# One linear-attention and two-MoE kernel: weight pieces pinned on GpSimd's queue, half of the next x split in place, g's affine moved to y's eviction

## The chip, the cores and the metric

One Trainium2 chip (trn2), one NeuronCore. The metric is device time of one execution in microseconds, given as the median of several runs. Lower is better.

## The reference, cut to what matters

```python
q_s = softmax(q, axis=-1)                 # per token and head, 4 x 8 x 576 x 64
k_s = softmax(k, axis=2)                  # over the sequence
kv  = einsum('bhsd,bhse->bhde', k_s, v)
x   = einsum('bhsd,bhde->bhse', q_s, kv)  # to 2304 tokens x 512
h   = x @ moe_w_in                        # 512 -> 2048
r   = maximum(h, 0)
g   = s * (r * r) + b                     # s and b are single numbers
x2  = g @ moe_w_out                       # 2048 -> 512
h2  = x2 @ moe2_w_in
out = (h2 * tanh(softplus(h2))) @ moe2_w_out
```

The weights come as float64, so the kernel first makes float32 of their bit halves. Products are made in float32r, each operand cut into a high and a low part (`split`: a cast on ScalarE, a subtraction on VectorE), with three matmuls for one product (`passes`).

## The kernel before, in words

**First MoE.** The tokens are cut into five chunks (512, 256, 512, 512, 512), and a step is one chunk c and one of 16 blocks f of 128 hidden units. In each step TensorE makes h of the step two ahead (`emit_h`, 12 matmuls), ScalarE makes r, r², and s·r²+b in three instructions (`emit_relu2`, L233 to L237) and splits g, and TensorE adds 12 matmuls into the four banks of y (`emit_y`). After 16 steps `y_out` copies y to SBUF and stores it to DRAM (yd). The attention for the next chunk, with its loads of kb, vb and q on SP's queue (SyncE), runs among these steps.

**Preparing the second MoE's weights.** The second MoE multiplies pairs of chunks, (0, 2) and (3, 4), by a scheme with seven products P1 to P7 in place of eight, and chunk 1 plainly (the rest). It needs sums of weight blocks, split into high and low. That is done during chunks 2 to 4 in 32 units: `unit_load` fetches 512 KB of raw weights into ur (one buffer, L288, on GpSimd's queue, the profile's POOL); `unit_sums` makes float32 of it (`bits`: ACT L128, then DVE L129, L132, L136, L140), starts the next unit's load, and forms the block sums (L299); `unit_split` splits them into umem and stores them to DRAM (wdi for w_in, wdo for w_out, POOL L312). ACT's instruction L128 and the casts are held in program order with ACT's relu L233 (`keep_in_program_order`); the rest of the order is chosen by a scheduler that simulates the program.

**Second MoE.** For a pair, `b_load` fetches the y blocks, `b_sums` makes the seven inputs x of P1 to P7 and splits them. For pair 0 this is done in place (`put_slot`), for pair 1 through DRAM (`put_dram` stores, `x_get` fetches 1 MB per product at L375). Then eight `h_unit` (42 matmuls each, s sums L436, mish L439), and `y_pair`, which goes over the seven products, each with eight blocks F. The split weights come from DRAM in pieces of up to 1 MB through a ring of three buffers (`ring_load`, tile rw, POOL L395 and L398): a piece is asked for when the one three before it has been used. `rest_load` (L563, L566) fetches the pieces for chunk 1. All these loads are on POOL's queue, in the order that the scheduler gives them. An instruction that issues a DMA waits there for its buffer, and what stands behind it waits too.

Of the kernel before, what the change touches and what calls it, by code (L numbers as in the profile page):

```python
# [31 lines left out]
def kernel(  # L32
# [191 lines left out]
    def emit_relu2(m):  # L224

        n = CHUNKS[steps[m][0]]
        if whole_y(m):
            r = gp.tile([P, CM], F32, tag="gl", name=f"r{m}")[:, 0:n]
            g_t[m] = (None, r)
        else:  # L230
            r = rp.tile([P, CM], F32, tag="r", name=f"r{m}")[:, 0:n]
            g_t[m] = g_tiles(m, n)
        op = nc.scalar.activation(out=r, in_=h_ps.pop(m), func=AF.Relu)  # L233
        if m >= U0:
            tc.keep_in_program_order(op)
        nc.scalar.activation(out=r, in_=r, func=AF.Square)
        nc.scalar.activation(out=r, in_=r, func=AF.Identity, scale=sb_s, bias=sb_b)  # L237
        if not whole_y(m):
            split(*g_t[m], r)

    def emit_y(n):
# [6 lines left out]
        for m in range(NK):  # L248
            ps = y_ps[c][m][:, 0:nt]
# [6 lines left out]
    def y_out(c):  # L256
        w = CHUNKS[c]
        for m, ps in enumerate(y_ps.pop(c)):
# [19 lines left out]
    def unit_load(e):  # L278
# [38 lines left out]
    events = [(fn, e) for e in range(len(units)) for fn in (unit_sums, unit_split)]  # L317

    def unit_event(i):
        fn, e = events[i]  # L320
        fn(e)

# [593 lines left out]
    for n in range(NS):  # L916
# [111 lines left out]
```

## Time and profile before

| | |
|---|---|
| median of 3 runs | 911.91 us (909.95 to 914.84) |
| the profiled execution | 908.81 us, span 907.0 us |
| TensorE (PE) busy | 839.7 us, 93% of the span |
| VectorE (DVE) busy | 619.2 us, 68% |
| ScalarE (ACT) busy | 491.6 us, 54% |
| GpSimd (POOL) busy | 130.7 us, 14% |
| DMA | 186.36 MB, mean 205 GB/s |
| mean granted TensorE clock | 0.981 |

By time: up to 30 us the first loads, chunk 0 to about 141 us, chunk 1 to 208, chunk 2 to 322, chunk 3 to 419, chunk 4 to 526; pair 0's `h_unit`s to 598, its `y_pair` to 683; pair 1's to 767 and 847; the rest to 907. A busy PE includes matmuls at half clock, so the shares are read with the granted clock and with the number of matmuls that started in a stretch.

### The profile page before, as it was taken

To read this page: it belongs to the slowest core of one execution; us is meant where nothing else is said; L and a number is where in the kernel's file an instruction comes from. 1 tells how busy PE (TensorE), PEld (TensorE's weight loads), DVE (VectorE), ACT (ScalarE), POOL (GpSimd) and SP (SyncE) were. 2 spreads that over 40 slices of the span, in tenths; PEclk is the share of its full clock that TensorE was granted. 3 is DMA by queue.
4 is the path that set the end of the run, shared out by engine and by line. 5 is a ranking of instruction groups with operands and counts; after the bars stand their busy time and mean duration, and the time that the engine had idled before them with its cause. 6 is when DMAs were issued, how large, how long until landed. Compare 5 with 4: busy or idle time off the path is not lost.

```text
span 907.0 us, 11652 instructions
## 1 busy us (share of the span) xinstructions
PE 839.7 (93%) x4084; PEld 667.4 (74%) x4084; DVE 619.2 (68%) x1147; ACT 491.6 (54%) x864; POOL 130.7 (14%) x212
## 2 busy tenths in 40 slices
PE   4799998999999898998988988987999999699998
PEld 3344887998877677786865777776788888578897
DVE  7888987666777866676669667864865656386511
ACT  4666886776667765675667644443443333344422
POOL 4000000000112122222221201120011112000110
PEclk9999999999999899999999999998999999899999
DMA  7992123123655466667674599997556768955791
GB/s 198 326 379 59 34 73 110 52 63 99 209 178 179 137 239 233 210 196 248 205 226 148 180 327 323 360 401 272 173 189 217 213 196 262 352 185 186 229 304 47
DMA packets 87498, 186.36 MB, mean 205 GB/s; under 512 B 27152, under 2 KB 45328, under 8 KB 82960
## 3 DMA queue, kind: packets, MB, share of 16 engines
q0 software_dynamic: 33968, 133.18, 45.2%
q1 hardware_dynamic: 52384, 51.40, 17.8%
q10 hardware_dynamic: 1088, 1.05, 0.4%
q8 instruction: 32, 0.52, 0.2%
q14 instruction: 26, 0.21, 0.1%
HBM read 135.27 MB, written 50.33 MB: 205 GB/s over the span
## 4 chain that ended last, share of the span: by engine, by line
PE 45%; DMA 21%; DVE 18%; issue 7%; ACT 7%; POOL 1%; SPq 1%; POOLq 0%; ACTq 0%; DVEq 0%
PE P L176 15%; PE h L176 6%; DMA ur<-in_moe_w_in_dram 5%; PE y L176 4%; DMA rw<-wdo 4%; PE h L212 4%; DMA ur<-in_moe_w_out_dram 4%; PE y L252 3%; PE rh L176 3%; PE ry L176 2%; DVE u L140 2%; DVE u L136 2%; DVE g L340 2%; DMA b<-yd 2%; ACT u L128 1%
## 5 line engine op out<-in xcount | busy, mean ns | idle before, releaser
L176 PE MATMUL h<-xh,w 128*128 128x512 f32 (+1 forms) x568 | 180.0, 382 | 13.9 <-ACT r L233 13.3
L176 PE MATMUL y<-gh,w 128*128 128x512 f32 (+1 forms) x584 | 177.1, 370 | 0.9 <-ACT gh L169 0.9
L176 PE MATMUL P<-xoP,rw 128*128 128x512 f32 x672 | 157.0, 391 | 6.9 <-DMA rw<-wdi 5.6
L176 PEld LDWEIGHTS P<-xoP,rw 128*128 128x128 f32 x672 | 125.1, 188 | 35.2 <-issue 5.6
L176 PEld LDWEIGHTS h<-xh,w 128*128 128x128 f32 x568 | 106.6, 194 | 36.6 <-ACT r L233 17.7
L169 ACT CAST ghy_P<-g 128x512 fp32r<-128x512 f32 x112 | 69.7, 623 | 104.0 <-DVE gly_P L166 34.7
L176 PEld LDWEIGHTS y<-gh,w 128*128 128x128 f32 x584 | 106.5, 189 | 20.2 <-ACT gh L169 2.2
L166 DVE TENSOR_TENSOR gly_P<-g,ghy_P 128x512 fp32r<-128x512 f32 x112 | 76.2, 690 | 60.5 <-ACT ghy_P L169 59.8
L176 PE MATMUL y<-gl,w 128*128 128x512 f32 (+1 forms) x292 | 106.8, 368 | 0.8 <-DVE gl L166 0.8
L176 PE MATMUL h<-xl,w 128*128 128x512 f32 (+1 forms) x284 | 106.6, 376 | 0.6 <-DVE xl L166 0.6
L176 PE MATMUL P<-ghy_P,rw 128*128 128x512 f32 x224 | 89.5, 401 | 14.4 <-DMA rw<-wdo 14.4
L436 DVE TENSOR_TENSOR s<-s,P 128x512 f32<-128x512 f32 x112 | 74.7, 685 | 39.5 <-PE P L176 28.0
L439 ACT ACTIVATE g<-s 128x512 f32<-128x512 f32 x64 | 39.8, 632 | 76.2 <-DVE s L436 75.7
L176 PEld LDWEIGHTS y<-gl,w 128*128 128x128 f32 x292 | 55.0, 188 | 10.3 <-DVE gl L166 1.6
L176 PEld LDWEIGHTS h<-xl,w 128*128 128x128 f32 x284 | 55.3, 195 | 9.7 <-DVE xl L166 1.0
L237 ACT ACTIVATE r<-r,sb_b,sb_s 128x512 f32<-128x512 f32 (+1 forms) x80 | 60.8, 770 | 1.4
L176 PEld LDWEIGHTS P<-ghy_P,rw 128*128 128x128 f32 x224 | 43.3, 193 | 24.4 <-issue 15.9
L166 DVE TENSOR_TENSOR gl<-r,gh 128x512 fp32r<-128x512 f32 (+1 forms) x73 | 45.6, 628 | 20.4 <-ACT gh L169 20.1
L169 ACT CAST umem<-u 128x512 fp32r<-128x512 f32 x64 | 37.3, 618 | 37.7 <-DVE u L299 32.7
L233 ACT ACTIVATE r<-h 128x512 f32<-128x512 f32 (+1 forms) x80 | 43.0, 549 | 20.8 <-PE h L176 14.3
L288 POOL DMA_DIRECT2D ur<-in_moe_w_in_dram x16 | 11.7, 734 | 270.2 <-DVE u L299 124.6
L166 DVE TENSOR_TENSOR umem<-u,umem 128x512 fp32r<-128x512 f32 x64 | 42.2, 688 | 12.3 <-ACT umem L169 12.1
(180 smaller groups left out, 1400.5 us busy)
## 6 DMA issues: line engine op xcount, KB each, us to landing
rw<-wdo POOLq DMA_DIRECT2D x28, 1024.0 KB, 5.1
wdi<-umem POOLq DMA_DIRECT2D x32, 512.0 KB, 4.0
rw<-wdi POOLq DMA_DIRECT2D x16, 1024.0 KB, 6.8
wdo<-umem POOLq DMA_DIRECT2D x32, 512.0 KB, 4.3
rw<-wdi POOLq DMA_DIRECT2D x16, 768.0 KB, 6.8
raw<-in_moe_w_in_dram SPq DMA_DIRECT2D x16, 512.0 KB, 9.9
raw<-in_moe_w_out_dram SPq DMA_DIRECT2D x16, 512.0 KB, 10.7
ur<-in_moe_w_in_dram POOLq DMA_DIRECT2D x16, 512.0 KB, 4.6
```

Source lines behind the costliest of these rows:

```text
L136: nc.vector.scalar_tensor_tensor(out=ti, in0=high, scalar=-0x40000000, in1=ti, op0=ALU.bitwise_and, op1=ALU.bitwise_or,)
L140: nc.vector.scalar_tensor_tensor(out=ti, in0=low, scalar=29, in1=ti, op0=ALU.logical_shift_right, op1=ALU.bitwise_or,)
L166: eng.tensor_tensor(out=lo, in0=src, in1=hi.bitcast(F32), op=ALU.subtract)
L169: pin(nc.scalar.copy(out=hi, in_=src))
L176: mm = nc.tensor.matmul(out=ps, lhsT=x, rhs=y, start=start, stop=stop)
L212: nc.tensor.matmul(out=h_ps[m], lhsT=wl[:, o], rhs=x_whole[kk], start=kk == 0, stop=kk == NK - 1,)
L233: op = nc.scalar.activation(out=r, in_=h_ps.pop(m), func=AF.Relu)
L237: nc.scalar.activation(out=r, in_=r, func=AF.Identity, scale=sb_s, bias=sb_b)
L252: nc.tensor.matmul(out=ps, lhsT=wl[:, o], rhs=gl, start=f == 0, stop=False)
L340: nc.vector.tensor_tensor(out=t.rearrange("p (a b) n -> p b a n", b=2)[:, 1], in0=t[:, 1:3], in1=t[:, 0:1].to_broadcast([P, 2, CM]), op=AL ...
L436: nc.vector.tensor_tensor(out=out, in0=a, in1=b, op=ALU.add)
L439: nc.scalar.activation(out=g[:, spot], in_=src, func=AF.Mish)
```

## The change

1. The units' raw loads go from GpSimd's queue to SP's. A unit's sums and its split are placed half a step apart, and the units evenly in half steps (slots "early" at the start of a step and "unit" at its end).
2. `ring_load`, `rest_load` and the load in the new `put_both` are held in program order on POOL's queue.
3. Pair 1's x: only k block 0 goes through DRAM (3.5 MB written and read in place of 7). k block 1 is split in place by `put_both`, one product at a time after each product of pair 0's `y_pair` in the program text; that function also fetches block 0's half (512 KB).
4. ACT's instruction s·r²+b (L237) goes. y's eviction multiplies by s, and adds b times a column sum of w_out: for chunk 1, g is made two columns of ones wider, so that y's bank has the column sums in two more columns; from these `bsum` is taken. Chunks 1 to 4 add it at eviction, chunk 0 in `b_steps` of pair 0 (four DVE instructions).

```diff
+    bsum = const.tile([P, NK], F32, name="bsum")
...
-            r = rp.tile([P, CM], F32, tag="r", name=f"r{m}")[:, 0:n]
-            g_t[m] = g_tiles(m, n)
+            wide = n + (2 if steps[m][0] == 1 else 0)
+            full = rp.tile([P, CM], F32, tag="r", name=f"r{m}")[:, 0:wide]
+            r = full[:, 0:n]
+            g_t[m] = g_tiles(m, wide)
+            if wide > n:
+                nc.gpsimd.memset(full[:, n:wide], 1.0)
         op = nc.scalar.activation(out=r, in_=h_ps.pop(m), func=AF.Relu)
         if m >= U0:
             tc.keep_in_program_order(op)
         nc.scalar.activation(out=r, in_=r, func=AF.Square)
-        nc.scalar.activation(out=r, in_=r, func=AF.Identity, scale=sb_s, bias=sb_b)
         if not whole_y(m):
-            split(*g_t[m], r)
+            split(*g_t[m], full)
...
         for m in range(NK):
-            ps = y_ps[c][m][:, 0:nt]
+            ps = y_ps[c][m][:, 0:nt + (2 if c == 1 else 0)]
...
-            (nc.vector.tensor_copy if m % 2 else nc.scalar.copy)(out=ys, in_=ps[:, 0:w])
+            b = bsum[:, m:m + 1]
+            if c == 1:
+                nc.vector.tensor_scalar(out=b, in0=ps[:, w:w + 1], scalar1=sb_b, scalar2=None, op0=ALU.mult)
+            if c == 0:
+                nc.scalar.activation(out=ys, in_=ps[:, 0:w], func=AF.Copy, scale=sb_s)
+            elif m % 2:
+                nc.vector.tensor_scalar(
+                    out=ys, in0=ps[:, 0:w], scalar1=sb_s, scalar2=b, op0=ALU.mult, op1=ALU.add
+                )
+            else:
+                nc.scalar.activation(out=ys, in_=ps[:, 0:w], func=AF.Identity, scale=sb_s, bias=b)
             nc.sync.dma_start(out=y_dram[c][:, m, :], in_=ys)
...
-    x_dram = {r: dram.tile([P, 2, 2, CM], F32, name=f"xd{r}") for r in H_ORDER}
+    x_dram = {r: dram.tile([P, 2, CM], F32, name=f"xd{r}") for r in H_ORDER}
...
-        nc.gpsimd.dma_start(out=raw.rearrange("p (j f) -> p j f", j=2), in_=src)
+        nc.sync.dma_start(out=raw.rearrange("p (j f) -> p j f", j=2), in_=src)
...
+    def b_steps(pair, kb, put):
         t = b_raw.pop(kb)
-        put("P1", kb, t[:, 0])
-        diff3(t)
-        put("P7", kb, t[:, 3])
-        put("P2", kb, t[:, 1])
-        sum2(t)
-        put("P6", kb, t[:, 0])
-        diff41(t)
-        put("P5", kb, t[:, 3])
-        put("P4", kb, t[:, 1])
-        put("P3", kb, t[:, 2])
-
-    def x_slot(r):
-        x_op[r] = wp.tile([P, 2, 2, CM], F32R, tag=f"w{H_ORDER.index(r)}", name=f"xo{r}")
+        if pair == 0:
+            for spot in range(2):
+                b = bsum[:, 2 * spot + kb:2 * spot + kb + 1]
+                nc.vector.tensor_scalar(out=t[:, spot], in0=t[:, spot], scalar1=b, scalar2=None, op0=ALU.add)
+        for r in Y_ORDER:
+            if r == "P7":
+                diff3(t)
+            elif r == "P6":
+                sum2(t)
+            elif r == "P5":
+                diff41(t)
+            put(r, kb, t[:, SPOT[r]])
+            yield
+
...
-            nc.sync.dma_start(out=x_dram[r][:, i, kb], in_=t.bitcast(F32))
-
-    def x_get(r):
-        x_slot(r)
-        nc.gpsimd.dma_start(out=x_op[r], in_=x_dram[r])
+            nc.sync.dma_start(out=x_dram[r][:, i], in_=t.bitcast(F32))
+
+    def put_both(r, kb, src):
+        x_op[r] = wp.tile([P, 2, 2, CM], F32R, tag=f"w{H_ORDER.index(r)}", name=f"xo{r}")
+        pin(nc.gpsimd.dma_start(out=x_op[r][:, :, 1 - kb], in_=x_dram[r]))
+        split(x_op[r][:, 0, kb], x_op[r][:, 1, kb], src)
...
-            nc.gpsimd.dma_start(out=t[:, :, 0:o.stop - o.start], in_=wi_dram[a][:, :, o])
+            pin(nc.gpsimd.dma_start(out=t[:, :, 0:o.stop - o.start], in_=wi_dram[a][:, :, o]))
         else:
             t = t.rearrange("p i f h d -> p (i f h d)")
-            nc.gpsimd.dma_start(out=t, in_=wo_dram[b][:, BLOCK[a]].rearrange("p f i h d -> p (f i h d)"))
+            pin(nc.gpsimd.dma_start(out=t, in_=wo_dram[b][:, BLOCK[a]].rearrange("p f i h d -> p (f i h d)")))
...
-            nc.gpsimd.dma_start(out=t, in_=wi_dram[F][:, :, 3:7])
+            pin(nc.gpsimd.dma_start(out=t, in_=wi_dram[F][:, :, 3:7]))
...
-    for i in range(len(events)):
-        at(U0 + i * (U1 - U0) // len(events), "unit", unit_event, i)
+    for e in range(len(units)):
+        i = 2 * (U1 - U0) * e // len(units)
+        for d, fn in enumerate((unit_sums, unit_split)):
+            at(U0 + (i + d) // 2, ("early", "unit")[(i + d) % 2], fn, e)
     for kb in range(2):
         at(L0 + 8, "load", b_load, 0, kb, f"w{NU + kb}")
-        at(L0 + 10 + kb, "unit", b_sums, kb, put_slot)
+        at(L0 + 10 + kb, "unit", b_all, 0, kb, put_slot)
...
-            elif F in (1, 3, 5):
-                if F > 1:
-                    b_sums(F // 2 - 1, put_dram)
-                if F < 5:
-                    b_load(1, F // 2, "w7")
+            elif F in (1, 5):
+                b_load(1, F // 4, "w7")
+            elif F == 3:
+                b_all(1, 0, put_dram)
         if pair == 0:
-            more = [(x_get, r) for r in H_ORDER]
+            steps_b = b_steps(1, 1, put_both)
+            more = [(next, steps_b)] * 7
```

**POOL's queue, start of pair 0's `y_pair`.** rw is a ring piece (here of wdo), xoP the x of pair 1; the names' numbers are buffers. Before:

```order
L398 DMA rw_5368<-wdo_101 128x2048
L375 DMA xoP_5538<-xdP_103 128x2048
L375 DMA xoP_5632<-xdP_104 128x2048
L375 DMA xoP_5724<-xdP_105 128x2048
L398 DMA rw_5406<-wdo_102 128x2048
L375 DMA xoP_5818<-xdP_106 128x2048
L375 DMA xoP_5910<-xdP_107 128x2048
L375 DMA xoP_6002<-xdP_108 128x2048
L398 DMA rw_5438<-wdo_101 128x2048
L375 DMA xoP_6092<-xdP_109 128x2048
```

With the change:

```order
L411 DMA rw_5268<-wdo_102 128x2048
L411 DMA rw_5306<-wdo_103 128x2048
L411 DMA rw_5338<-wdo_102 128x2048
L411 DMA rw_5392<-wdo_103 128x2048
L411 DMA rw_5436<-wdo_102 128x2048
L387 DMA xoP_5438<-xdP_104 128x2x512
```

Six xoP loads of 1 MB that stood between the first three pieces are gone from there; the first piece of x, now of half the size, stands behind the fifth.

**POOL's queue, start of pair 1's `y_pair`.** rw_wi and rw_wo are the rest's pieces. Before:

```order
L398 DMA rw_6626<-wdo_101 128x2048
L563 DMA rw_wi_6815<-wdi_93 128x2x1024
L563 DMA rw_wi_6909<-wdi_94 128x2x1024
L563 DMA rw_wi_7095<-wdi_95 128x2x1024
L398 DMA rw_6671<-wdo_102 128x2048
L566 DMA rw_wo_7001<-wdo_101 128x4x512
L566 DMA rw_wo_7187<-wdo_101 128x4x512
L563 DMA rw_wi_7277<-wdi_96 128x2x1024
L398 DMA rw_6703<-wdo_101 128x2048
L398 DMA rw_6769<-wdo_102 128x2048
```

With the change:

```order
L411 DMA rw_6543<-wdo_102 128x2048
L411 DMA rw_6588<-wdo_103 128x2048
L411 DMA rw_6620<-wdo_102 128x2048
L411 DMA rw_6686<-wdo_103 128x2048
L411 DMA rw_6730<-wdo_102 128x2048
L576 DMA rw_wi_6732<-wdi_94 128x2x1024
L411 DMA rw_6780<-wdo_103 128x2048
L411 DMA rw_6824<-wdo_102 128x2048
L576 DMA rw_wi_6826<-wdi_95 128x2x1024
```

Six of the rest's pieces that stood ahead of the third ring piece stand behind later ones, one after two ring pieces.

**SP's queue, start of chunk 2, with the change.** ur is a unit's raw weights; kb, vb, q are the attention's loads, yd stores y. Before, the same loads stand in the same queue without the ur, which stood on POOL's.

```order
L647 DMA kb<-in_k_dram 128x2x256
L280 DMA yd_90<-ys_1_2135 128x256
L651 DMA kb<-in_k_dram 64x2x64
L667 DMA vb<-in_v_dram 128x4x64 x2
L302 DMA ur_2220<-in_moe_w_in_dram 128x2x512
L671 DMA vb<-in_v_dram 64x2x64
L302 DMA ur_2340<-in_moe_w_in_dram 128x2x512
L685 DMA q_3_2605<-in_q_dram 112x2x256
L685 DMA q_3_2605<-in_q_dram 16x2x256
L647 DMA kb<-in_k_dram 128x2x256
L651 DMA kb<-in_k_dram 64x2x64
L302 DMA ur_2421<-in_moe_w_in_dram 128x2x512
```

A ur now stands behind loads that wait for the attention's buffers.

**DVE, around pair 0's last `h_unit`.** s_0_7 are its seven sums, gly_P_3 the low part that the fourth block of `y_pair`'s first product needs. Before:

```order
L436 TENSOR_TENSOR s_0_7_5371<-s_0_7_5370,P_0_7_5382 128x512
L436 TENSOR_TENSOR s_0_7_5372<-s_0_7_5371,P_0_7_5390 128x512
L436 TENSOR_TENSOR s_0_7_5371<-s_0_7_5371,P_0_7_5398 128x512
L436 TENSOR_TENSOR s_0_7_5370<-s_0_7_5370,P_0_7_5408 128x512
L436 TENSOR_TENSOR s_0_7_5370<-s_0_7_5372,P_0_7_5398 128x512
L436 TENSOR_TENSOR s_0_7_5372<-s_0_7_5372,P_0_7_5417 128x512
L436 TENSOR_TENSOR s_0_7_5371<-s_0_7_5371,P_0_7_5428 128x512
L334 TENSOR_TENSOR g_7_5373<-g_7_5373 128x512
L166 TENSOR_TENSOR gly_P_3_5482<-g_3_4998,ghy_P_3_5481 128x512
```

With the change (the first 12 of 18 rows up to gly_P_3; the other six are three xoP subtractions, the last sum, a difference of g, and gly_P_3; L345 and L348 on b_1 are the sum and the difference that L337 and L340 were):

```order
L449 TENSOR_TENSOR s_0_7_5271<-s_0_7_5270,P_0_7_5282 128x512
L167 TENSOR_TENSOR xoP_5438<-b_1_5195,xoP_5438 128x512
L345 TENSOR_TENSOR b_1_5195<-b_1_5195 128x512
L449 TENSOR_TENSOR s_0_7_5272<-s_0_7_5271,P_0_7_5290 128x512
L167 TENSOR_TENSOR xoP_5726<-b_1_5195,xoP_5726 128x512
L449 TENSOR_TENSOR s_0_7_5271<-s_0_7_5271,P_0_7_5298 128x512
L167 TENSOR_TENSOR xoP_5535<-b_1_5195,xoP_5535 128x512
L449 TENSOR_TENSOR s_0_7_5270<-s_0_7_5270,P_0_7_5308 128x512
L167 TENSOR_TENSOR xoP_5629<-b_1_5195,xoP_5629 128x512
L348 TENSOR_TENSOR b_1_5195<-b_1_5195 128x2x512
L449 TENSOR_TENSOR s_0_7_5270<-s_0_7_5272,P_0_7_5298 128x512
L449 TENSOR_TENSOR s_0_7_5271<-s_0_7_5271,P_0_7_5328 128x512
```

Seven subtractions for xoP, one sum and one difference of b, nine instructions, now stand among the seven sums ahead of gly_P_3.

## Rows read from the trace of the kernel before

**Rows 1.** By stretch: busy us (instructions) of PE, PEld, DVE, ACT, POOL; granted clock, DMA share, GB/s.

```profile
144.00:208.00 64.00, 61.84 (x529) 58.64 (x528) 41.30 (x104) 44.30 (x105) 0.00 (x0) 1.00 0.28 76
419.00:526.00 107.00, 96.23 (x399) 76.18 (x399) 74.57 (x148) 67.82 (x112) 24.53 (x33) 0.97 0.63 204
683.00:767.00 84.00, 84.00 (x383) 69.48 (x382) 49.37 (x76) 27.82 (x46) 16.01 (x24) 1.00 0.73 210
```

**Rows 2.** PE's waits over the whole run: us in total, times, longest us.

```profile
PE P L176 <- DMA rw<-wdo: 14.4, 4, 5.1
PE h L176 <- ACT r L233: 13.3, 11, 3.6
...
PE P L176 <- DMA rw<-wdi: 5.6, 3, 2.4
PE x L176 <- DVE qtl L166: 3.9, 1, 3.9
```

**Rows 3.** The chain of waits, 369 to 378 us: start, us, what.

```profile
369.74 4.29 DMA ur<-in_moe_w_out_dram
...
374.11 0.68 ACT u L128
...
376.46 0.70 DVE u L140
...
377.20 0.52 issue
377.73 4.30 DMA ur<-in_moe_w_out_dram
```

**Rows 4.** DMA issues: KB each, median us from issue to landing.

```profile
ur<-in_moe_w_out_dram POOLq DMA_DIRECT2D x16, 512.0 KB, 4.3
...
out_dram<-os SPq DMA_DIRECT2D x8, 512.0 KB, 3.0
...
rx<-yd SPq DMA_DIRECT2D x1, 512.0 KB, 6.1
```

**Rows 5.** By stretch, as rows 1, for 10 us each.

```profile
420.00:430.00 10.00, 6.43 (x22) 4.82 (x21) 6.16 (x14) 5.03 (x9) 2.24 (x3) 0.85 0.78 267
480.00:490.00 10.00, 8.69 (x37) 6.50 (x36) 10.00 (x19) 5.95 (x11) 0.71 (x1) 1.00 0.30 96
592.00:602.00 10.00, 10.00 (x46) 8.28 (x45) 5.47 (x10) 3.16 (x6) 4.20 (x8) 1.00 1.05 393
```

**Rows 6.** Groups of instructions by line, ACT, 208 to 526 us: busy us, mean ns.

```profile
L237 ACT ACTIVATE r<-r,sb_b,sb_s 128x512 f32<-128x512 f32 x48 | 38.3, 812 | 0.8
```

**Rows 7.** Timeline of PE: start, us, line, instruction [idle before, releaser].

```profile
494.22 0.50 PE L176 MATMUL h<-xh,w 128*128 128x512 f32 x1 [2.46 <-ACT r L233]
```

**Rows 8.** The chain of waits, 590 to 630 us.

```profile
598.76 18.08 DMA rw<-wdo
```

**Rows 9.** By stretch, as rows 1, start of both y_pairs.

```profile
600.00:610.00 10.00, 7.74 (x35) 6.09 (x34) 7.11 (x12) 3.73 (x6) 0.53 (x1) 1.00 1.07 427
610.00:620.00 10.00, 4.89 (x16) 3.68 (x15) 1.92 (x3) 2.31 (x5) 0.53 (x1) 0.73 1.09 420
620.00:630.00 10.00, 10.00 (x42) 8.12 (x42) 5.21 (x7) 4.26 (x7) 0.53 (x1) 0.93 0.51 184
770.00:780.00 10.00, 5.30 (x17) 3.97 (x16) 4.36 (x7) 1.61 (x3) 0.54 (x1) 0.75 1.20 407
780.00:790.00 10.00, 7.69 (x31) 5.92 (x30) 4.00 (x6) 3.71 (x7) 0.53 (x1) 0.90 1.14 414
```

**Rows 10.** Timeline of DVE, as rows 7.

```profile
601.93 1.38 DVE L166 TENSOR_TENSOR gly_P<-g,ghy_P 128x512 fp32r<-128x512 f32 x2 [1.29 <-ACT ghy_P L169]
```

**Rows 11.** SP queue's own waits: us in total, times, longest us.

```profile
SPq L672 <- DVE qn L740: 91.5, 11, 18.4
SPq L654 <- PE kv L760: 50.2, 10, 16.3
...
SPq L634 <- DVE ke L717: 35.9, 7, 17.3
```

More of the change, by code (lines that the diff above doesn't have):

```diff
@@ L227, in emit_relu2 @@
         if whole_y(m):
-            r = gp.tile([P, CM], F32, tag="gl", name=f"r{m}")[:, 0:n]
+            r = full = gp.tile([P, CM], F32, tag="gl", name=f"r{m}")[:, 0:n]
             g_t[m] = (None, r)
         else:
-            r = rp.tile([P, CM], F32, tag="r", name=f"r{m}")[:, 0:n]
-            g_t[m] = g_tiles(m, n)
+            wide = n + (2 if steps[m][0] == 1 else 0)
[4 more added lines that the diff above has]
+                nc.gpsimd.memset(full[:, n:wide], 1.0)
         op = nc.scalar.activation(out=r, in_=h_ps.pop(m), func=AF.Relu)
@@ L315, in unit_split @@
             )
[L317 to L321, printed above, removed]
     b_raw, x_op = {}, {}
@@ L343, in diff41, with b_all @@
         )
-    def b_sums(kb, put):
+    def b_steps(pair, kb, put):
         t = b_raw.pop(kb)
-        put("P1", kb, t[:, 0])
-        diff3(t)
-        put("P7", kb, t[:, 3])
-        put("P2", kb, t[:, 1])
-        sum2(t)
-        put("P6", kb, t[:, 0])
-        diff41(t)
-        put("P5", kb, t[:, 3])
-        put("P4", kb, t[:, 1])
-        put("P3", kb, t[:, 2])
-    def x_slot(r):
-        x_op[r] = wp.tile([P, 2, 2, CM], F32R, tag=f"w{H_ORDER.index(r)}", name=f"xo{r}")
+        if pair == 0:
[11 more added lines that the diff above has]
+            yield
+    def b_all(pair, kb, put):
+        for _ in b_steps(pair, kb, put):
+            pass
     def put_slot(r, kb, src):
         if kb == 0:
-            x_slot(r)
+            x_op[r] = wp.tile([P, 2, 2, CM], F32R, tag=f"w{H_ORDER.index(r)}", name=f"xo{r}")
         split(x_op[r][:, 0, kb], x_op[r][:, 1, kb], src)
@@ L370, in put_dram @@
         for i, t in enumerate((hi, lo)):
-            nc.sync.dma_start(out=x_dram[r][:, i, kb], in_=t.bitcast(F32))
-    def x_get(r):
-        x_slot(r)
-        nc.gpsimd.dma_start(out=x_op[r], in_=x_dram[r])
+            nc.sync.dma_start(out=x_dram[r][:, i], in_=t.bitcast(F32))
+    def put_both(r, kb, src):
+        x_op[r] = wp.tile([P, 2, 2, CM], F32R, tag=f"w{H_ORDER.index(r)}", name=f"xo{r}")
+        pin(nc.gpsimd.dma_start(out=x_op[r][:, :, 1 - kb], in_=x_dram[r]))
+        split(x_op[r][:, 0, kb], x_op[r][:, 1, kb], src)
     ring, ring_at = [], [0, 0]
@@ L562, in rest_load @@
         if z == "wi":
-            nc.gpsimd.dma_start(out=t, in_=wi_dram[F][:, :, 3:7])
+            pin(nc.gpsimd.dma_start(out=t, in_=wi_dram[F][:, :, 3:7]))
         else:
             t = t.rearrange("p i b h d -> p (i b h d)").rearrange("p (b i h d) -> p b i h d", b=4, i=2, h=2)
-            nc.gpsimd.dma_start(
+            pin(nc.gpsimd.dma_start(
                 out=t.rearrange("p b i h d -> p b (i h d)"),
                 in_=wo_dram[F // 4][:, 3:7, F % 4].rearrange("p b i h d -> p b (i h d)"),
-            )
+            ))
             t = t.rearrange("p b i h d -> p i b h d")
@@ L922 @@
         boundary = any(steps[m][1] == 0 for m in hs)
-        run(n, "att5", "att2", "att3")
+        run(n, "att5", "att2", "att3", "early")
         if n < NF:
```

## The prediction

> **What bounds the kernel now.** I read the time by stretch first, then TensorE's waits, then the chain of waits in the stretches that lose time. PE is busy nearly throughout, and in pair 1's h_units it has no idle time at all [rows 1]. So the kernel is bounded by matmuls plus the stretches where PE starves, and only these can give time. A full 10 us holds 46 matmuls of 512 columns (592 to 602) [rows 5], that is 0.217 us each. PE's waits name three kinds of starving [rows 2].
>
> First, ring pieces: PE waits for rw<-wdo 14.4 us in four waits, two at the start of each y_pair, and 5.6 us in three waits for rw<-wdi in pair 0's h_units. Second, the relu of the next step: 13.3 us in 11 waits. Third, one wait of 3.9 us on the attention's qtl.
>
> The second kind comes from the weight units. In chunks 3 and 4 the chain of waits runs round a loop [rows 3]: ur is fetched in 4.29 us, one ACT and four DVE instructions take it to 377.20, and 0.52 us after these comes the next fetch, 8.0 us after the last. There is one ur buffer, so no fetch starts earlier. 32 units are spread over 45 steps of 24 matmuls, so a unit has 45/32 x 24 x 0.217 = 7.3 us where nothing else runs. The loop is slower than that. The unit falls behind, ACT's L128 waits for ur in its fixed place, and the relu stands behind it. Where PE waits long, the granted clock then falls: 420 to 430 us holds 22 matmuls instead of 46, at a clock of 0.85 [rows 5].
>
> **The change part by part.** The sum is made against the profiled execution, 908.8 us, which is 3.1 us under the median of 911.9 that the forecast is scaled to.
>
> *ur on SP's queue.* Removed: 32 issues on POOL. Added: 32 issues on SP, among the loads of kb, vb and q and the y stores. No row shows this transfer on SP. The nearest rows bound it: 512 KB on SP landed in 3.0 us (out_dram<-os) and in 6.1 us (rx), against 4.3 us for ur on POOL [rows 4]. I take 3.2, nearer the first, since that is a median of eight and the other a single one. The loop then takes 8.0 - 4.3 + 3.2 = 6.9 us, below 7.3, and the units keep pace. Of the 13.3 us of relu waits one of 2.5 us, at 494 [rows 7], lies behind a stretch in which DVE is 10.00 us busy out of 10 [rows 5]. The other 10.8 us go. In the clock I count 2.5 us: the stretch 420 to 430 lost 24 matmuls, 5.2 us, of which at most 3.6 us is its wait, so 1.6 us is slow matmuls, and one other wait was long enough for something like it. The qtl wait lies among the same crowd of unit work on DVE; I count half, 2.0 us. Total 15.3 us.
>
> *L237 removed.* 48 instructions, 38.3 us, leave ACT in chunks 2 to 4 [rows 6]. ACT is 67.8 of 107 us busy in chunk 4 [rows 1], so nearly all of it is off the path and costs nothing now; it shortens the time from h to gh. Four additions of bsum come into the DVE-full stretch near 480. The loop's two short DVE instructions of the same shape take 377.20 - 374.11 = 3.1 us less 0.68 (ACT) and two of 0.70, so 0.5 us each [rows 3]; four make 2.0 us. That stretch costs PE 4.5 us: 37 matmuls instead of 46 from 480 to 490 [rows 5], 2.0 us, and the wait of 2.5 us after it [rows 7]. I count 2.0 us of it gained net of the additions, since the unit and relu work comes earlier, and keep 0 and 4 as ends. The eviction is still one instruction for each bank.
>
> *Columns of ones.* 12 matmuls in each of 16 steps, 192, are 258 wide instead of 256: 192 x 2/512 x 0.217 = 0.2 us lost. The 16 memsets go to POOL, which is 0.00 us busy in chunk 1 [rows 1]; nothing as long as no other work stands there.
>
> *Pinned ring pieces.* The chain at 598.76 waits 18.08 us for a piece that was issued behind six xoP loads of 1 MB [rows 8], and pair 1's start looks alike with rest pieces in their place. Full stretches would hold 138 and 92 matmuls in the 30 and 20 us shown; there are 93 and 48 [rows 9]. So 45 x 0.217 = 9.8 us and 44 x 0.217 = 9.6 us are lost, waits and half-clock matmuls together. With the pieces first in the queue nothing of 1 MB stands ahead of the second and third piece, and I take both losses back. What is late next in pair 0 is DVE, below.
>
> *k block 1 split in place.* Removed: 14 stores of 256 KB on SP's queue and half of the seven xoP loads. In pair 0's h_units, where PE waited 5.6 us for rw<-wdi, I count two of the three waits, 3.1 us; the longest, 2.4 us, stays, since it comes before the stores of this block would. Added around the last h_unit, ahead of gly_P_3: nine DVE instructions, one of them twice as wide. Ten take 5.47 us there now [rows 5], so these take ten times 0.55, 5.5 us. DVE is idle for 10 - 5.47 = 4.5 us in the same stretch. gly_P_3 starts at 601.93 [rows 10], about when PE wants it; so it comes 5.5 - 4.5 = 1.0 us late. I count 1.0 us lost, with 0 and 3 as ends (the casts beside them go to ACT, busy for 3.16 of those 10 us).
>
> *Sum.* 15.3 + 2.0 - 0.2 + 9.8 - 1.0 + 9.6 + 3.1 = 38.6 us. 908.8 - 38.6 = 870.2 for a profiled execution, and 911.9 - 38.6 = **873.3, so 873 us** as a median.
>
> **The rivals.**
>
> *ur is no faster on SP (R1).* If the transfer takes 4.3 us there too, the loop stays at 8.0 us and the relu waits and their clock, 13.3 us, stay: 873.3 + 13.3 = 887 us. For it speaks that rx took 6.1 us [rows 4]; against it, the out_dram row. The Trainium skill has a rule for this: DMA: Bandwidth & Descriptors, section Issuing engines are not separate DMA queues, says that DMAs from all issuing engines run on the same 16 engines, and that another issuer saves only issue time. By that rule the sum would be about 25 us. The rows of 4.3 and 3.0 us for 512 KB lean the other way, though they are not the same transfer.
>
> *ur waits behind SP's other work (R2, slower).* SP's queue waits 91.5 + 50.2 + 35.9 = 178 us on the attention's buffers [rows 11], and the order puts ur behind some of these loads. A load whose buffer is not free holds ur and then ACT's relu. Each us of mean delay is 32 us of loop, after a slack of 0.4 x 32 = 13 us. It undoes the sum from 13 + 39 = 52 us of the 178 on, and is slower by over 0.5% from 56 us on; at half of the 178 the time is 873 + 89 - 13 = 949 us. Against it: the order places a ur only where the DVE work that frees the load ahead comes before that which frees the ur, and in the last chunk and a half hardly anything but ur stands there. The bound of 6.1 us for the transfer would give the same: a loop of 9.8 us, 2.5 x 32 = 80 us, 953 us.
>
> *DVE becomes the bound (R3).* The burst costs 3 instead of 1 us, the qtl wait and the stretch near 480 give nothing (4.0 us), and the bsum additions cost their 2.0 us: 873 + 8 = 881 us. DVE's 10.00 of 10 speaks for it [rows 5]; that ACT work leaves, and that the full stretch is one of few, against.
>
> **How the numbers follow.** Forecast 0.60, R1 0.20, R3 0.15, R2 0.05. Low end: the whole qtl wait (2), the whole of the 480 stretch (2), no burst loss (1), the third h_unit wait (2.4) and as much clock again elsewhere (6) give 860. High end: R1 with most of R3's 8 us, 894. That leaves out R2 and some 0.1 at both ends. What a measurement can tell here is about 0.5%, 4.6 us. Forecast, R1 and R3 are all faster by more; some of their chance goes to cases that mix R1, R3 and a little of R2. Faster 0.92, same 0.03, slower 0.05.
>
> **What would show it.** Right: ur lands in about 3.2 us and its issues come 7.3 us apart or more, PE's waits for the relu fall from 13.3 to about 2.5 us, its waits for rw<-wdo go, a short wait on gly appears at the start of pair 0's y_pair, and the first 30 us of that stage hold above 130 matmuls. Wrong: ur landing in 4 us or more, or issue waits of SP in front of ur (R1, R2), a DVE at 10 of 10 with PE waiting on it (R3), or pieces that PE still waits for, which would mean that the landing itself, and not the place in the queue, was the limit.

## The result, and the profile after

The changed kernel takes 882.07 us (median of 4, 879.26 to 888.89) against 910.93 us before (median of 4). The ratio is 0.9688, 95% interval 0.9623 to 0.9752: faster, by 28.9 us. Forecast were 873 us and a range of 860 to 894. So the sign and the range held, and 9 us of the expected gain are missing. The profiled execution took 882.98 us, span 881.2 us, mean granted clock 0.986; before it was 908.81 and 907.0.

First the starts of both y_pairs, by stretch of 10 us, in the profile after the change (columns as in [rows 1]; the first three lines answer to pair 0's in [rows 9], the others to pair 1's):

```profile
590.00:600.00 10.00, 8.99 (x40) 7.10 (x40) 9.97 (x17) 6.76 (x12) 1.06 (x2) 1.00 0.62 198
600.00:610.00 10.00, 10.00 (x46) 8.28 (x45) 6.66 (x11) 5.44 (x10) 1.78 (x3) 1.00 0.73 250
610.00:620.00 10.00, 10.00 (x46) 8.15 (x45) 8.47 (x11) 4.42 (x8) 1.22 (x2) 1.00 0.75 245
740.00:750.00 10.00, 10.00 (x45) 8.27 (x45) 5.84 (x9) 3.10 (x6) 1.08 (x2) 1.00 0.69 215
750.00:760.00 10.00, 10.00 (x46) 8.26 (x45) 9.16 (x15) 6.34 (x10) 1.06 (x2) 1.00 0.69 230
```

They are full but for six matmuls in the first, where DVE is 9.97 of 10 us busy. PE's waits over the whole run, after (us in total, times, longest; lines that no reading here rests on are left out):

```profile
...
PE h L177 <- ACT r L238: 8.6, 5, 4.5
PE P L177 <- DVE s L449: 3.6, 1, 3.6
PE P L177 <- DMA rw<-wdi: 3.2, 2, 3.0
...
PE P L177 <- DVE gly_P L167: 1.9, 3, 1.0
```

Against [rows 2], the wait for rw<-wdo is gone, the relu waits fell from 13.3 to 8.6 us, and a wait for a sum s, 3.6 us, is new. Two regions still lose time. By stretch, after:

```profile
450.00:460.00 10.00, 5.51 (x18) 4.08 (x17) 5.39 (x12) 5.09 (x9) 1.50 (x2) 0.83 0.86 279
460.00:470.00 10.00, 9.36 (x41) 7.09 (x39) 9.97 (x21) 5.33 (x10) 0.00 (x0) 1.00 0.82 271
470.00:480.00 10.00, 7.16 (x24) 5.53 (x25) 10.00 (x19) 6.70 (x12) 1.50 (x2) 0.83 0.33 114
480.00:490.00 10.00, 8.29 (x37) 6.55 (x36) 8.31 (x19) 6.65 (x12) 1.49 (x2) 1.00 0.54 160
520.00:530.00 10.00, 6.21 (x26) 4.55 (x25) 3.89 (x7) 2.52 (x5) 0.71 (x1) 0.89 0.99 327
530.00:540.00 10.00, 10.00 (x36) 7.99 (x35) 8.78 (x14) 5.32 (x10) 1.41 (x2) 0.77 0.86 293
540.00:550.00 10.00, 7.01 (x27) 5.38 (x27) 7.38 (x13) 3.03 (x6) 0.70 (x1) 0.91 0.97 323
```

To count where the time went, I took every 10 us from the start of chunk 2 to the end of pair 1's y_pair that hold fewer than 44 matmuls, and counted what is missing to 46, at 0.217 us each:

| stretch | lost before | lost after | gained | forecast |
|---|---|---|---|---|
| chunks 2 to 4 | 30.6 | 18.2 | 12.4 | 17.3 |
| pair 0's h_units | 6.5 | 11.5 | -5.0 | 3.1 |
| pair 0's y_pair | 11.3 | 2.8 | 8.5 | 8.8 |
| pair 1's y_pair | 11.5 | 1.5 | 10.0 | 9.6 |
| sum | 59.9 | 34.1 | 25.8 | 38.8 |

The spans differ by 907.0 - 881.2 = 25.8 us, so the table accounts for the change (the forecast's 0.2 us for the wider matmuls has no row, and short matmuls of the attention count like others, so a stretch of chunk 2 can hide a loss).

### The profile page after: what moved, and what is told of

Same layout as the page of the kernel before. It is cut to its first block, busy times and chain, and to the rows that moved or that the text cites. A ratio compares the mean times of both kernels' runs of the same rounds, so it can differ in the third digit from the quotient of the medians.

```text
span 881.2 us, 11571 instructions
## 1 busy us (share of the span) xinstructions
PE 835.9 (95%) x4084; PEld 667.9 (76%) x4084; DVE 621.2 (70%) x1153; ACT 440.7 (50%) x786; POOL 109.4 (12%) x196
## 4 chain that ended last, share of the span: by engine, by line
PE 48%; issue 30%; DVE 12%; POOL 5%; DMA 3%; ACT 2%; SPq 0%; POOLq 0%; DVEq 0%; ACTq 0%
PE P L177 20%; PE h L213 4%; PE h L177 4%; PE y L177 3%; PE rh L177 3%; PE ry L177 3%; POOL wdo L326 2%; PE y L256 2%; DVE g L348 2%; POOL wdi L326 2%; DVE gly_P L167 1%; PE P3y L177 1%; PE P5y L177 1%; PE P7y L177 1%; PE P4y L177 1%
## 5 line engine op out<-in xcount | busy, mean ns | idle before, releaser
L177 PE MATMUL h<-xh,w 128*128 128x512 f32 (+1 forms) x568 | 176.7, 376 | 9.9 <-ACT r L238 8.6
L177 PE MATMUL P<-xoP,rw 128*128 128x512 f32 x672 | 161.4, 398 | 9.2 <-DVE s L449 3.6
L177 PEld LDWEIGHTS P<-xoP,rw 128*128 128x128 f32 x672 | 128.4, 192 | 38.5 <-DVE s L449 4.0
L177 PEld LDWEIGHTS h<-xh,w 128*128 128x128 f32 x568 | 105.0, 191 | 30.5 <-ACT r L238 11.3
L177 PE MATMUL P<-ghy_P,rw 128*128 128x512 f32 x224 | 87.0, 390 | 0.0
L167 DVE TENSOR_TENSOR umem<-u,umem 128x512 fp32r<-128x512 f32 x64 | 42.4, 689 | 11.1 <-ACT umem L170 10.9
L241 ACT ACTIVATE r<-r 128x512 f32<-128x512 f32 (+1 forms) x80 | 47.0, 589 | 1.5
L177 PE MATMUL P<-gly_P,rw 128*128 128x512 f32 x112 | 45.2, 404 | 2.3 <-DVE gly_P L167 1.9
## 6 DMA issues: line engine op xcount, KB each, us to landing
raw<-in_moe_w_out_dram SPq DMA_DIRECT2D x16, 512.0 KB, 10.8
```

Source lines behind the costliest of these rows:

```text
L167: eng.tensor_tensor(out=lo, in0=src, in1=hi.bitcast(F32), op=ALU.subtract)
L177: mm = nc.tensor.matmul(out=ps, lhsT=x, rhs=y, start=start, stop=stop)
```

## The experiments

All times are medians of 4 executions; ratios are to the kernel before, with their 95% intervals. Every edit makes the scheduler place the program anew, so besides the time each run's own waits are read. The changed kernel's own four executions lie 9.6 us apart. By the spread of the four times on each side, a difference to it is known to about 6.5 us (an estimate): those of 8.7 to 12.8 us below stand clear of that, the 8.7 barely, and those of 2.5, 3.9 and 4.9 us do not.

**Parts undone, one at a time.**

*ur back on GpSimd's queue.*

```diff
-        nc.sync.dma_start(out=raw.rearrange("p (j f) -> p j f", j=2), in_=src)
+        nc.gpsimd.dma_start(out=raw.rearrange("p (j f) -> p j f", j=2), in_=src)
```

> The units' raw loads go back to GpSimd's queue, everything else as changed. Theory C (the move to SP's queue keeps the units in pace): relu waits rise from 8.6 to 15 us or more, and the time rises to about 891 us. Rival (the removed ACT instruction and the new places of sums and splits did it, since ur lands in 3.8 to 4.2 us on SP against 4.3 us on GpSimd's queue): relu waits stay under 11 us and the time within 3 us of 882.

891.57 us, 0.9801 (0.9767 to 0.9835); relu waits 18.9 us. Theory C holds: this part is worth 9.5 us. Two fetches one after the other in chunk 4 of this run, where nothing else holds up the loop (chain of waits: start, us, what):

```profile
426.51 4.16 DMA ur<-in_moe_w_out_dram
...
434.35 4.08 DMA ur<-in_moe_w_out_dram
```

The loop is 7.8 us here. With the change, a loop of chunk 4 that nothing else holds up (SP's and DVE's timelines: start, us):

```profile
418.18 0.38 SPq L302 DMA_DIRECT2D ur<-in_moe_w_out_dram  x1
...
424.36 0.69 DVE L141 SCALAR_TENSOR_TENSOR u<-ur,u 128x512 int32<-128x512 int32 x1
...
425.11 0.38 SPq L302 DMA_DIRECT2D ur<-in_moe_w_out_dram  x1
```

That is 6.9 us. SP issues the next load 0.06 us after DVE's last instruction on ur, where POOL takes some 0.56 us; the other 0.4 us is the landing, counted from the start of the issue. DMA issues (KB, median us to landing), of the change and then of this run:

```profile
ur<-in_moe_w_in_dram SPq DMA_DIRECT2D x16, 512.0 KB, 4.2
ur<-in_moe_w_out_dram SPq DMA_DIRECT2D x16, 512.0 KB, 3.8
```

```profile
ur<-in_moe_w_in_dram POOLq DMA_DIRECT2D x16, 512.0 KB, 4.6
ur<-in_moe_w_out_dram POOLq DMA_DIRECT2D x16, 512.0 KB, 4.2
```

*No load pinned on GpSimd's queue.* `pin` goes from all five loads in `ring_load`, `rest_load` and `put_both`, as here:

```diff
-        pin(nc.gpsimd.dma_start(out=x_op[r][:, :, 1 - kb], in_=x_dram[r]))
+        nc.gpsimd.dma_start(out=x_op[r][:, :, 1 - kb], in_=x_dram[r])
```

> No load on GpSimd's queue is held in program order, everything else as changed. Theory D (the order of the ring pieces is worth what was lost at the start of both y_pairs): waits for rw<-wdo return to 10 us or more and the time rises to about 900 us. Rival (in pair 0 halving the x loads is enough by itself): only pair 1's start loses its 9 to 10 us again, and the time is about 892 us.

891.75 us, 0.9797 (0.9767 to 0.9827), as the rival had it. Only pair 1's start loses again; PE's wait there, in total 6.2 us:

```profile
PE P L177 <- DMA rw<-wdo: 6.2, 3, 3.9
```

These waits are at 761 and 772 us; pair 0's y_pair has none. In pair 0 six xoP loads again stand between the first three ring pieces on POOL's queue, the last three of them here, each of 512 KB and not of 1 MB:

```profile
587.79 0.57 POOL L411 DMA_DIRECT2D rw<-wdo  x1 [0.66 <-PE P L177]
588.35 0.70 POOL L387 DMA_DIRECT2D xoP<-xdP  x1
590.05 1.40 POOL L387 DMA_DIRECT2D xoP<-xdP  x2 [1.00 <-PE P L177]
591.87 0.57 POOL L411 DMA_DIRECT2D rw<-wdo  x1 [0.41 <-PE P L177]
```

So with this order the halved bytes are enough to clear the start. Pinning is worth 9.7 us: pair 1's y_pair loses 10.9 us here against 1.5 with the change.

*Both k blocks of pair 1's x through DRAM*, with the kernel before's loads of b and its stores of both blocks.

```diff
-            steps_b = b_steps(1, 1, put_both)
-            more = [(next, steps_b)] * 7
+            more = [(x_get, r) for r in H_ORDER]
...
+        pin(nc.gpsimd.dma_start(out=x_op[r], in_=x_dram[r]))
```

> Both k blocks of pair 1's x go through DRAM again (7 MB each way), one load of 1 MB after each product, in program order behind the ring pieces; everything else as changed. Theory G (with the pieces in order, halving the x loads adds nothing at the start of pair 0's y_pair): no wait for rw<-wdo there, the wait for gly goes, waits for rw<-wdi in pair 0's h_units rise from 3.2 to about 5.5 us, and the time is 881 to 886 us. Rival (the halved bytes are what cleared that start): waits for rw<-wdo of 5 us or more return in pair 0's y_pair and the time is about 892 us.

884.57 us, 0.971 (0.9654 to 0.9767): within Theory G's range, 2.5 us over the change, which is not clear of the noise. No wait for rw<-wdo appears, and the wait for gly at the start of pair 0's y_pair is gone. The waits for rw<-wdi did not rise: of 3.1 us in all, 0.5 us are in pair 0's h_units, though the 14 stores are back, and 2.7 us at 695 us, in pair 1's. Taken with the run before, pair 0's start is cleared by either part alone, the order or the halved bytes.

*s·r²+b back on ACT*; the two columns, bsum and its additions go, and y is evicted by plain copies.

```diff
         nc.scalar.activation(out=r, in_=r, func=AF.Square)
+        nc.scalar.activation(out=r, in_=r, func=AF.Identity, scale=sb_s, bias=sb_b)
```

> s times r squared plus b goes back to ACT (80 instructions), and with it the columns of ones, bsum and its four additions go; everything else as changed. Theory E (ACT is not on the path, the removed instruction is worth about nothing): relu waits stay at 11 us or less and the time within 3 us of 882. Rival (the relief of ACT is what lets the relu come in time): relu waits return to 13 us or more and the time is 888 us or more.

890.78 us, 0.978 (0.9729 to 0.9832); relu waits:

```profile
PE h L177 <- ACT r L238: 12.2, 6, 6.9
```

The rival holds by the time and nearly by the waits: with everything that the edit moves, this part is worth 8.7 us. That it is ACT's 0.8 us a step is not shown. Chunks 2 and 3, with 32 of the 48 instructions, lose 3.9 us here against 4.3 with the change, counted as in the table. The loss is in chunk 4: 4.1 us from 410 to 420 and 21.3 us against 13.9 from 450 to 500 us. The longest relu wait, 6.9 us at 461 us, stands behind a cast for pair 0's x that waits for b (ACT):

```profile
452.58 0.66 ACT L129 ACTIVATE u<-ur 128x512 f32<-128x512 f32 x1 [4.73 <-DMA ur<-in_moe_w_out_dram]
458.94 0.62 ACT L170 CAST xoP<-b 128x512 fp32r<-128x512 f32 x1 [5.71 <-DMA b<-yd]
...
460.51 0.59 ACT L238 ACTIVATE r<-h 128x512 f32<-128x512 f32 x1
```

With the change this cast comes behind the relu. The instruction and the order that the scheduler gives ACT for it were not told apart.

*The units' old places.*

```diff
-        i = 2 * (U1 - U0) * e // len(units)
-        for d, fn in enumerate((unit_sums, unit_split)):
-            at(U0 + (i + d) // 2, ("early", "unit")[(i + d) % 2], fn, e)
+    for i, (fn, e) in enumerate(events):
+        at(U0 + i * (U1 - U0) // len(events), "unit", fn, e)
```

> The units' sums and splits go back to the kernel before's places (64 events spread over whole steps), everything else as changed. Theory H (the half-step places matter little, the other parts add up to 30.4 us already): within 3 us of 882. Rival (a split one half step behind its sums keeps the relu free): relu waits of 13 us or more and 887 us or more.

869.25 us, 0.9555 (0.9511 to 0.96). Neither expectation was right: undoing this part saves 12.8 us. Relu waits nearly vanish (the one line of PE's waits):

```profile
PE h L177 <- ACT r L238: 0.7, 2, 0.4
```

ACT's timeline shows the difference at the same place, a ur that lands late while the first ring pieces load. With the change (start, us, instruction, idle before it and releaser):

```profile
450.01 0.66 ACT L129 ACTIVATE u<-ur 128x512 f32<-128x512 f32 x1 [5.16 <-DMA ur<-in_moe_w_out_dram]
453.81 1.29 ACT L170 CAST umem<-u 128x512 fp32r<-128x512 f32 x2 [3.13 <-DVE u L313]
455.00 0.59 ACT L238 ACTIVATE r<-h 128x512 f32<-128x512 f32 x1
```

In the run with the old places:

```profile
444.84 0.66 ACT L129 ACTIVATE u<-ur 128x512 f32<-128x512 f32 x1 [6.52 <-DMA ur<-in_moe_w_out_dram]
445.41 0.59 ACT L238 ACTIVATE r<-h 128x512 f32<-128x512 f32 x1
...
449.12 1.14 ACT L170 CAST umem<-u 128x512 fp32r<-128x512 f32 x2 [1.81 <-DVE u L313]
```

In both, ACT waits for ur. With the change, what stands next is the same unit's casts, which wait for eight DVE instructions on that ur, and the relu only after them: from ur's landing to the relu 5.0 us. With the old places the relu stands right behind L129, 0.6 us after the landing. When sums fall at a step's end, a split half a step later is at the next step's start, ahead of its relu. In ACT's program order, the casts follow L129 without a relu between in 16 of 32 units with the change, in 10 with the old places, in 12 before. Not all of the 12.8 us is this: chunk 2 and 3's losses fell by 4.3 us, but the DVE-full stretch, now at 440 to 480 us, still loses 12.6 us, and about 5.6 us come from pair 0's h_units, where the scheduler here put y's stores ahead of b's loads. DVE still waits 6.3 us for b there, at 519 us, but PE's longest wait for a sum is 1.5 us.

**The two regions that still lose time.**

*First ring pieces spread.*

```diff
-        at(L0 + 4, "load", ring_load)
+        at(L0 + 2 * i, "load", ring_load)
```

> The three first ring pieces are asked for two steps apart from step 64 on, instead of all three in step 68. Theory A (the pinned burst of 2.75 MB at 437.7 us made one unit's weights land in 9.1 instead of 3.8 us, ACT waited 5.2 us and the relu 4.5 us at 455.6): that landing falls to 5 us or less, the wait of 4.5 us goes, and the time falls from 882 to about 877 us. Rival (the additions and subtractions for pair 0's x fill DVE and would cost the same anyway): of the 14 us of matmul time missing between 450 and 490 us at least 10 stay, and the time stays within 2 us of 882.

878.19 us, 0.9647 (0.9622 to 0.9672). Mixed: the longest ur landing fell from 9.1 to 6.6 us and the relu wait of 4.5 us to 2.3, but 13.7 of the 13.9 us in 450 to 490 stayed lost, as the rival had it. The next line shows it, waiting on xoP now. What less is lost is in chunk 2 and pair 0's h_units; the 3.9 us are not clear of the noise.

```profile
470.00:480.00 10.00, 4.31 (x8) 1.88 (x8) 9.61 (x19) 3.35 (x6) 0.00 (x0) 0.71 0.17 52
```

*y's stores and b's loads in order on SP.* The SP queue with the change, from 507 us, where chunk 4's y is stored and read back:

```profile
507.70 0.32 SPq L280 DMA_DIRECT2D yd<-ys  x1
513.59 0.32 SPq L338 DMA_DIRECT2D b<-yd  x1
513.96 1.40 SPq L280 DMA_DIRECT2D yd<-ys  x3
521.77 0.32 SPq L338 DMA_DIRECT2D b<-yd  x1
```

and DVE at that time:

```profile
526.11 0.69 DVE L342 TENSOR_TENSOR b<-b 128x512 f32<-128x512 f32 x1 [6.91 <-DMA b<-yd]
```

A load waits for the first store to land, and three stores stand behind it; the last load waits for these, and DVE for it, with the sums of h_unit queued behind. The edit:

```diff
-            nc.sync.dma_start(out=y_dram[c][:, m, :], in_=ys)
+            pin(nc.sync.dma_start(out=y_dram[c][:, m, :], in_=ys))
...
-        nc.sync.dma_start(out=t[:, spot], in_=y_dram[c][:, kk, :])
+        pin(nc.sync.dma_start(out=t[:, spot], in_=y_dram[c][:, kk, :]))
```

> The stores of y and the loads of b are held in program order on SP's queue, so that no load of chunk 4's y stands ahead of a store of it. Theory B (a load that waits for the first store holds up the other three stores, so the last b lands late, DVE stands 6.9 us at a difference of b, and PE waits 3.6 us for a sum at 529 us): DVE's wait falls to 2 us or less, PE's wait of 3.6 us goes, the 20 us from 520 to 540 hold about 90 matmuls instead of 62, and the time falls from 882 to about 877 us. Rival (y is simply ready too late for where DVE's order has the difference): DVE still waits 5 us or more and the time stays within 2 us of 882.

877.15 us, 0.9637 (0.961 to 0.9664). Theory B holds by its waits; the 4.9 us are not clear of the noise. The four stores now come first:

```profile
508.26 3.41 SPq L280 DMA_DIRECT2D yd<-ys  x4
512.32 1.78 SPq L338 DMA_DIRECT2D b<-yd  x4
```

DVE's wait is 0.2 us, the wait of 3.6 us is gone, and 520 to 540 us hold 80 matmuls instead of 62. That the order alone did it is not shown, since the transfers got shorter too. From 505 to 515 us, in the change and then in this run:

```profile
yd<-ys SPq DMA_DIRECT2D x4, 256.0 KB, 6.6
```

```profile
yd<-ys SPq DMA_DIRECT2D x4, 256.0 KB, 2.2
```

With the change a ring piece is loading while these stores run (issued at 506.5, landed after 6.8 us, the next issued at 513.7); here the last piece had landed before the first store. With the old places y's stores come first as well, and DVE waits 6.3 us.

*Both edits*, the last two diffs together.

> The first ring pieces spread over steps 64, 66 and 68, and y's stores and b's loads in program order on SP's queue, together. If the two cost separate waits, the savings of 3.9 and 4.9 us add up: about 873 us. Rival (both runs still lost 11 us or more of matmul time in the stretch where DVE is full, and part of each saving was the same): 876 us or more.

876.4 us, 0.9632 (0.9587 to 0.9676): the rival, by less than the noise. From 480 to 510 us this run still loses 11.7 us, in the DVE-full stretch and right behind it, where PE waits for one relu:

```profile
495.87 0.79 PE L177 MATMUL P<-xoP,rw 128*128 128x512 f32 x1 [6.05 <-ACT r L238]
```

The run with y's stores in order alone has the same wait, 5.7 us at 496. In both, ACT comes to this relu right after L129 and the casts of one unit, which waited 3.3 us for DVE. So the relu wait of 4.5 us that the change has at 455 us shrank, and another behind casts grew: relu waits are 8.6 us with the stores in order and 9.3 with both, against 8.6 with the change.

*With both, units from step 26 to 73.*

```diff
-        i = 2 * (U1 - U0) * e // len(units)
+        i = 2 * (UB - UA) * e // len(units)
...
-            at(U0 + (i + d) // 2, ("early", "unit")[(i + d) % 2], fn, e)
+            at(UA + (i + d) // 2, ("early", "unit")[(i + d) % 2], fn, e)
```

UA is U0 - 6 and UB is L0 + NF - 7.

> As the run with both, and the weight units are placed from step 26 to step 73 instead of 32 to 77. Theory F (what is left between 450 and 500 us comes from unit work and pair 0's x products meeting on DVE): the matmul time lost there falls from 11 us or more to 5 us or less, and the time falls by about 6 us against the run with both. Rival (the x products fill DVE by themselves, or chunks 1 to 3 lose as much): within 2 us of the run with both.

874.7 us, 0.961 (0.9566 to 0.9654), within 2 us, as the rival had it. The loss near 450 to 500 fell to 5.6 us, as Theory F said, but the start of chunk 2 pays for it:

```profile
210.00:220.00 10.00, 4.52 (x32) 2.92 (x30) 8.56 (x21) 3.66 (x7) 1.07 (x2) 0.68 0.64 204
220.00:230.00 10.00, 6.73 (x19) 5.47 (x20) 9.20 (x25) 5.17 (x10) 1.07 (x2) 0.50 0.72 228
```

*With both, units from step 28 to 75*: UA is U0 - 4 and UB is L0 + NF - 5.

> As the run with both, and the units from step 28 to 75. Theory F: the 8.9 us that steps 26 on cost at the start of chunk 2 (210 to 230 us) shrink to 4 us or less, the stretch from 450 to 500 us loses 8 us or less, and the time is about 872 us. Rival (what is gained at one end is paid at the other): 874 to 877 us.

882.79 us, 0.9715 (0.9661 to 0.9768), a miss for both. The start of chunk 2 lost 4.1 us, about as expected, but 470 to 490 lost 9.8 and 520 to 550 lost 12.2 us, where DVE waited 5.3 us for b although the stores stood first. The trace shows the loads slow, not late in the queue: a ring piece was issued at 505.0, ahead of the stores, and landed in 6.2 us, the next in 10.0 us. Of the stores from 505 to 515 us:

```profile
yd<-ys SPq DMA_DIRECT2D x4, 256.0 KB, 5.5
```

So the order of stores and loads is not enough in these runs: it also counts whether a ring piece is loading at that time.

*With both, pair 0's x products spread.*

```diff
-        at(L0 + 10 + kb, "unit", b_all, 0, kb, put_slot)
+        for i in range(7):
+            at(L0 + 9 + kb + (i + kb) // 2, ("early", "unit")[(i + kb) % 2], b_next, kb)
```

Here `b_next` takes one step of `b_steps`.

> As the run with both, and pair 0's 14 x products are placed one or two in each half step from step 73 to 78, instead of seven in step 74 and seven in step 75. Theory I (the burst of x products is what fills DVE): the matmul time lost from 450 to 500 us falls from 11.5 to 6 us or less, and the time to about 871 us. Rival (the amount of DVE work counts, not its bunching, or the scheduler bunches it again): within 2 us of 876.

869.82 us, 0.9564 (0.9516 to 0.9613). Theory I holds; 450 to 490 us lose 5.4 us, all of it in the first three stretches:

```profile
450.00:460.00 10.00, 9.27 (x41) 7.64 (x42) 6.80 (x14) 7.28 (x14) 2.98 (x4) 1.00 0.69 227
460.00:470.00 10.00, 7.59 (x34) 6.00 (x33) 6.38 (x14) 3.15 (x7) 1.52 (x3) 1.00 0.81 239
470.00:480.00 10.00, 10.00 (x38) 8.10 (x38) 8.45 (x15) 8.19 (x16) 0.00 (x0) 0.83 0.54 210
```

The bunching was the cost, not the amount: the same products and additions, spread, cost 6 us less than in the run with both. The relu wait of 6.05 us went with it; the longest is 2.4 us. What is late next is a ring piece: 4.75 us for rw<-wdi at 513 us, issued behind the last unit's stores.

*With both, the x products spread and units from step 28 to 75.*

> Units from step 28 to 75 and the x products spread, with both other edits. If bunching and amount both count, the two savings add: about 868 us. If they are the same saving, no better than the better of the two alone.

870.75 us, 0.957 (0.9505 to 0.9635), no better than spreading alone: 450 to 500 us lose 0.9 us, but 220 to 230 us lose 5.0.

The two fastest versions thus beat the change by 12 to 13 us: the change with the old unit places, and the one with the x products spread and both small edits. They were not run together.

## Why the prediction was right and wrong

**y_pairs.** Right. The terms 9.8 - 1.0 and 9.6 us stand against 8.5 and 10.0 measured. The burst on DVE ahead of gly_P_3 was forecast at 1.0 us; the timeline of PE has

```profile
596.88 0.50 PE L177 MATMUL P<-gly_P,rw 128*128 128x512 f32 x1 [1.01 <-DVE gly_P L167]
```

and the first 30 us hold 132 matmuls (forecast: above 130). What I gave to the order alone has two causes in pair 0, each enough.

**"ur on SP's queue".** The loop of 6.9 us came true, by other terms, and the time that it had to fit in was mis-sized. ur lands in 3.8 to 4.2 us, not in 3.2: the rows I took as nearest were no guide, since in the changed kernel's profile out_dram<-os itself took 4.5 us and rx 3.2. By the transfer, R1 was nearer. Its time did not follow, as R1 took the loop to stay at 8.0 us. What made up for it is a term that the sum kept at POOL's size: with POOL 0.56 us pass between DVE's last instruction on ur and the next issue, with SP 0.06. So the rule of the Trainium skill, DMA: Bandwidth & Descriptors, section Issuing engines are not separate DMA queues, agrees: little more than issue time is saved, since the issue itself also got shorter (SP's 0.37 us against POOL's 0.71). The same page of the Trainium skill, section Latency and other measured facts, gives a first byte at about 0.6 us for SP's queue and about 1 us for GpSimd's. The 0.4 us between the two landing times is of that size, but the landing is counted from the issue's start and the issue accounts for most of it, so no run here shows it.

The time that a unit has, 7.3 us, was too short. It prices a matmul at 0.217 us, from 46 in 10 us, but two of these 46 are cut by the stretch's ends. PE's timeline of the kernel before has

```profile
730.52 31.82 PE L176 MATMUL P<-xoP,rw 128*128 128x512 f32 x139
```

which is 0.23 us each and 7.7 us for a unit. The loop of 7.8 us on POOL lies just above that and the one of 6.9 us on SP well below. That fits 0.9 us of loop being worth 9.5 us of kernel, though no run varied the time a unit has. Up to 430 us the losses fell from 18.9 to 4.3 us, by the three parts together that bear on the units; with ur back on POOL they are 13.5. R2 did not happen at ur: SP issued it within 0.34 us of DVE's last instruction in each of the 31 loops.

**"nearly all of it is off the path and costs nothing now".** Not borne out as a whole, and the cause stays open. With L237's instruction back the kernel takes 8.7 us more, where the sum had it at nothing but for the 2.0 us near 480. In chunks 2 and 3 the step holds: nothing is lost there for its return. In chunk 4 the relu waits grow, but the longest stands behind a cast that waits for b, and not behind this instruction. ACT's share, 67.8 of 107 us, could not show that: it is a mean, and the relu stands in a queue held in program order.

**The DVE-full stretch, "I count 2.0 us of it gained".** Wrong sign. From 450 on, chunk 4 lost 11.7 us before and loses 13.9 now. Of these, 6.1 us lie from 450 to 460, where the relu comes late behind a unit's casts before the first x product. Behind that the x products fill DVE (10.00 of 10), as R3 said, and the run that spreads them shows that it is their bunching. R3's 881 us is near the 882 measured by luck: its burst cost 1.0 and not 3 us, and the qtl wait, which it kept, fell from 3.9 to 0.3 us.

**The half-step places.** The prediction had no term for them. They stand behind most of the remaining relu waits, 8.6 us against the 2.5 forecast and 0.7 without them, and the part as a whole costs 12.8 us against the old places, though some 5.6 us of that come from pair 0's h_units. ACT's order, which the prediction left out, shows it: the waits of 4.5 and 1.7 us come right behind L129 and the casts of one unit.

**Pair 0's h_units, "two of the three waits, 3.1 us".** The number was near, the reason was not shown. rw<-wdi fell from 5.6 to 3.2 us, but with the 14 stores back, these waits are 0.5 us in pair 0's h_units, so it is not the stores that bring them about. And there is a new wait: the load of b in front of y's stores on SP, with a ring piece loading beside them, took 6.9 us of DVE and 3.6 us of PE, and the matmuls after it ran slow: 36 in 530 to 540 us at a clock of 0.77. In the kernel before, all four stores stand ahead of the two loads of this y. It is R2's mechanism, a blocked entry at the head of SP's queue, at another place than the prediction had it.

Undone one by one, the parts give 9.5 + 9.7 + 8.7 + 2.5 - 12.8 = 17.6 us; with the 9.8 us that the forecast has for pair 0's start, which either of two parts clears, 27.4 of the 28.9 us measured. Each of the five is known to some 6.5 us, so this sum is no proof that nothing is left out.

## What to carry to other kernels

An engine with a third of its time free still delays the bound engine if its queue is in program order and an instruction that waits stands ahead of one that is wanted: read the order between the waits, not the share. When loads and stores share a queue, look for a load that waits on the first of several stores and holds up the rest, and for what else is loading then. In a loop of load and work with one buffer, count the gap before the issue too, and set the loop against the time it has to fit in. A change of many parts can hide one that costs as much as another gains, so undo them one at a time.

## What the runs showed of the hardware

One kind of transfer is a poor price for another: 512 KB on SP's queue took 3.0 and 6.1 us (out_dram<-os, rx) in one profile [rows 4] and 4.5 and 3.2 us in the next, while the units' loads, made 32 times, moved by only 0.4 us between the two queues. The raw loads at the start of both kernels, 512 KB on SP's queue too, landed in 10.0 to 10.8 us.

From DVE's last instruction on a buffer to the issue of the load that waits for it, 0.56 to 0.58 us passed when GpSimd issued it (all 31 times in the kernel before) and 0.06 to 0.08 us when SyncE did (29 of 31 with the change, the longest 0.34).

A 256 KB store on SP's queue landed in 2.2 us (median of the four stores of chunk 4's y, with them in order on SP) when no ring piece was loading, and in 5.5 us (units from step 28 with both edits) and 6.6 us (the change) when one was.
